# Low halves of expert weights: from GpSimd to VectorE

## The chip, the cores and the metric

The kernel runs on one core of a Trainium2 chip. The metric is the device time of one launch in microseconds (us); three runs were made, and their median counts. Times of single instructions come from one profiled execution and count from the start of its span. The engines are called by the profile's names: PE (TensorE, its matmuls), PEld (TensorE's weight loads), DVE (VectorE), ACT (ScalarE), POOL (GpSimd) and SP (SyncE, which here issues most transfers). A q behind a name is the engine's queue.

## The reference

Three stages follow one another; all of it is fp32.

```python
# 1. a linear attention over 768 steps, 4 batches x 8 heads, heads of 64
state = gamma * state + k[t] (outer) v[t];  y[t] = scale * q[t] @ state
x = y as 3072 rows of 512
# 2. a mixture of experts: one of 8 experts for each row
logits = x @ w_gate + modality_bias[modality_id];  e_idx = argmax(logits)
h = relu(x[mask] @ w1[e])            # 512 -> 1024
out[mask] = gate_w[mask] * (h @ w2[e])   # 1024 -> 512
# 3. a second layer of the same kind; its gate_w is multiplied by a sigmoid gate
```

The data decide which row goes to which expert, and so how many rows an expert gets.

## The kernel before, in words

**Three products for one.** An fp32 operand is split into a high half, which is the operand rounded to a shorter type, and a low half, the rest. A product is then made as high x high + high x low + low x high. For the weights, ACT writes the high half (`w1h`, `w2h`; lines 505 and 510), and another engine subtracts it from the raw weights (`w1l`, `w2l`; lines 506 and 511): `los[i].tensor_tensor(w1l[i][:, cols], raw1[i][:, cols], w1h[i][:, cols], op=ALU.subtract)`. Which engine this is comes from a list `los` with one engine for each of the four tiles of a matrix. x and the hidden values are split too: `xh` and `xl` (lines 545 and 547), `hh` and `hl` (882 and 883, or 903 and 904); their low halves are made on DVE.

**Slots.** After the routing the rows of one expert lie together in memory. A slot is a block of up to 256 rows of one expert; a layer has 12 to 19 slots, of which those that exist are run. A slot of 256 rows is run by `run` (full); one with at most 128 rows by `run_small` (small): the last block of an expert that doesn't fill a slot. PE's work in a full slot is `mm1` (line 891, eight steps f) and `mm2` (line 909, eight steps j); in a small slot `mm1s` (line 896, four steps), a transposition back (`htr`, line 902), and `mm2` in four steps.

**When weights change.** A register of the slot says whether its expert differs from the slot before (`chg`) and whether the next slot's will differ (`chgn`). If the next one differs, `split1(0)` and `split1(1)` make that expert's w1h and w1l during the second half of the current slot, by half rows: block 0 has the first 512 columns of each of four tiles, block 1 the rest. The w2 of a new expert is split in the slot that uses it: in a full slot all four tiles at its start (`split2`, all on DVE), in a small slot in pieces between the steps of mm1s. The raw weights of the expert after that are fetched by SP as soon as the raw tiles have been read. Each layer's first slot splits its w2 by a list of its own, written in `run`.

**Order.** Each engine works its instructions off in the order of the code. `at(j)` puts in the routing of the previous slot's results to layer 2, in steps: PE transposes `ob` (line 939) and makes the logits (945, 952), DVE copies them (947: `lT`; 954: `r_lg`) and finds each row's expert (lines 186 to 210: `r_oh`), PE counts (215), DVE places (221 to 260), and POOL scatters the rows (469). In layer 2, POOL scatters the results to the output (919). `xpose` (line 540, DVE) and `xsplit` (545 on ACT, 547 on DVE) prepare the next slot's x between split1(0) and split1(1). In a small slot the hl of the second half (line 904) stands between split1(0) and xpose on DVE.

The part of `run_small` around it reads:

```python
if j == 0:
    self.split1(0)
if j == 1:
    self.coming(nxt, Slot.xpose)
    self.coming(nxt, Slot.xsplit)
    self.split1(1)
```

Of the kernel before, what the change touches and what calls it, by code (L numbers as in the profile page):

```python
# [416 lines left out]
def retention_moe_moe_kernel(ctx: ExitStack, tc: tile.TileContext, q, k, v, mod, mb, wg, wg2, w1, w2, cst_d, out):  # L417
    nc = tc.nc
# [83 lines left out]
    def split1(los, ks=range(KD), half=None):  # L502
        cols = slice(0, F) if half is None else slice(half * F // 2, (half + 1) * F // 2)
        for i in ks:
            nc.scalar.activation(w1h[i][:, cols], raw1[i][:, cols], AF.Copy)  # L505
            los[i].tensor_tensor(w1l[i][:, cols], raw1[i][:, cols], w1h[i][:, cols], op=ALU.subtract)  # L506
# [96 lines left out]
    with ExitStack() as actx:  # L603
# [126 lines left out]
        for i in range(n):  # L730
# [17 lines left out]
            if n - 4 <= i < n - 1:  # L748
                split1([nc.gpsimd] * KD, [i - n + 4] if i < n - 2 else [2, 3])
# [39 lines left out]
    with ExitStack() as mctx:  # L789
# [28 lines left out]
        class Slot:  # L818
# [102 lines left out]

            def split1(self, half=None):
                with tc.If(self.chgn > 0):
                    split1([nc.vector, nc.gpsimd] * 2, half=half)

            def split2(self, ks=range(4), los=None):
                with tc.If(self.chg > 0):
# [109 lines left out]
            def run_small(self, steps=(), nxt=()):  # L1037

                at = self.steps(steps)
                self.ids(False)  # L1040
                los = [nc.vector] * (1 + (self.li == 2)) + [nc.gpsimd] * 3
                self.split2((0,) if self.li == 1 else (0, 1), los)
                for j in range(4):
                    if j == 3:
                        self.htr(0)
                    at(j)
                    if j:
                        self.split2((((1,), (2, 3), ()), ((), (2,), (3,)))[self.li - 1][j - 1], los)
                    self.mm1s(j // 2, (2 * (j % 2), 2 * (j % 2) + 1))
                    if j % 2:  # L1050
                        nc.scalar.activation(hs[:, (j // 2) * 512:(j // 2 + 1) * 512], hT[j // 2], AF.Relu)
                for j in range(4):
                    if j == 1:
                        self.htr(1)
                        self.prepare()
                    at(4 + j)
# [7 lines that stand above are left out]
                        nc.vector.memset(self.o[:, 0, W - 1:], 0.0)  # L1064
                        if self.li == 2:
                            nc.gpsimd.memset(self.o[:, 0, W - 1:], 0.0)
                    self.mm2(1, range(2 * j, 2 * j + 2), False)
                self.done(1)
                at(8)
# [137 lines left out]
```

## Time and profile before

| | us |
|---|---|
| median of three runs (lowest, highest) | 864.4 (864.32, 865.25) |
| the profiled execution's own time | 863.35 |
| its span, first to last instruction | 861.6 |
| PE busy with matmuls | 799.3 |
| DVE busy | 432.6 |
| POOL busy | 278.6 |
| ACT busy | 276.7 |

The span is from the first to the last instruction; 1.75 us of the execution's own time lie around it. The attention takes up the first part. From about 170 us on, the two layers run: 30 slots, 24 full and six small ones, by the counts of lines 891 and 896 (768 and 48 matmuls of each of their three kinds, 32 in a full slot and 8 in a small one). Matmuls overlap in the records, so that one begins before the one before it has ended; the step from row to row is what a matmul takes of PE's time.

### The profile page before, as it was taken

What the parts mean: (1) busy time and instruction counts of PE and PEld (TensorE: products, weight loads), DVE (VectorE), ACT (ScalarE), POOL (GpSimd) and SP (SyncE); (2) the same over time, 40 slices, a digit from 0 to 9 for tenths busy, and PEclk for the clock granted to TensorE, in tenths of its full rate; (3) what the DMA queues carried; (4) which work ended last, traced back from release to release, by engine and by line L of the source; (5) the groups of instructions that cost most, each with busy time, mean ns of one, the idle gap of its engine ahead of it and who ended that gap; (6) DMA issues with size and microseconds to landing.
All of it is one profiled execution on the core that took longest, in us unless ns stands there. A gap on an engine that the chain in (4) does not pass through costs nothing. (4 is left out here: it accounts for less than half of the span.)

```text
span 861.6 us, 18471 instructions
## 1 busy us (share of the span) xinstructions
PE 799.3 (93%) x5987; PEld 694.8 (81%) x5987; DVE 432.6 (50%) x1065; ACT 276.7 (32%) x476; POOL 278.6 (32%) x336
## 2 busy tenths in 40 slices
PE   8999998799999988999999599998999999999892
PEld 7788877788888967888888377797888888888671
DVE  4554456743444447333446675235454763635821
ACT  3444445311112224111114441115151651514610
POOL 3455456701122114122211752014231531323810
PEclk9999999999999999999999889999999999999997
DMA  9987899272111116211221714412635475343410
GB/s 171 232 219 183 181 230 311 89 246 71 52 39 39 39 28 202 74 52 52 74 66 27 225 37 138 137 59 70 213 98 179 129 249 164 120 155 113 149 40 16
DMA packets 149692, 107.02 MB, mean 124 GB/s; under 512 B 94845, under 2 KB 125693, under 8 KB 149504
## 3 DMA queue, kind: packets, MB, share of 16 engines
q1 hardware_dynamic: 141664, 85.37, 37.4%
q0 software_dynamic: 6400, 18.98, 6.0%
q8 instruction: 73, 1.20, 0.6%
q14 instruction: 115, 0.94, 0.4%
q10 hardware_dynamic: 1440, 0.53, 0.3%
HBM read 167.64 MB, written 25.83 MB: 225 GB/s over the span
## 5 line engine op out<-in xcount | busy, mean ns | idle before, releaser
L891 PE MATMUL hT<-xh,w1h 128*128 128x256 f32 x768 | 221.9, 289 | 2.0 <-ACT xh L545 1.6
L891 PE MATMUL hT<-xh,w1l 128*128 128x256 f32 x768 | 216.4, 282 | 3.9 <-POOL w1l L506 3.9
L891 PE MATMUL hT<-xl,w1h 128*128 128x256 f32 x768 | 216.4, 282 | 1.5 <-DVE xl L547 1.4
L909 PE MATMUL po<-w2l,hh 128*128 128x512 f32 x432 | 171.9, 398 | 2.1 <-POOL w2l L511 2.1
L909 PE MATMUL po<-w2h,hh 128*128 128x512 f32 x432 | 172.9, 400 | 0.3
L891 PEld LDWEIGHTS hT<-xh,w1h 128*128 128x128 f32 x768 | 145.9, 190 | 9.7 <-issue 5.6
L891 PEld LDWEIGHTS hT<-xh,w1l 128*128 128x128 f32 x768 | 145.7, 190 | 4.7 <-POOL w1l L506 4.7
L891 PEld LDWEIGHTS hT<-xl,w1h 128*128 128x128 f32 x768 | 146.0, 190 | 3.5 <-DVE xl L547 2.6
L909 PE MATMUL po<-w2h,hl 128*128 128x512 f32 x432 | 136.4, 397 | 1.4 <-DVE hl L904 1.4
L883 DVE SCALAR_TENSOR_TENSOR hl<-hT,hh 128x512 fp32r<-128x512 f32 x96 | 65.6, 690 | 133.3 <-ACT hh L882 106.4
L882 ACT ACTIVATE hh<-hT 128x512 fp32r<-128x512 f32 x96 | 57.2, 597 | 197.9 <-PE hT L891 177.9
L506 POOL TENSOR_TENSOR w1l<-raw,w1h 128x512 fp32r<-128x512 f32 (+1 forms) x44 | 70.9, 1630 | 114.4 <-ACT w1h L505 114.4
L909 PEld LDWEIGHTS po<-w2h,hl 128*128 128x128 f32 x432 | 81.4, 189 | 22.3 <-DVE hl L904 2.4
L909 PEld LDWEIGHTS po<-w2l,hh 128*128 128x128 f32 x432 | 81.7, 189 | 20.9 <-POOL w2l L511 2.9
L909 PEld LDWEIGHTS po<-w2h,hh 128*128 128x128 f32 x432 | 81.8, 189 | 19.7 <-ACT hh L903 1.6
L469 POOL DMA_INDIRECT x2d<-ob,r_idx x28 | 30.4, 1086 | 183.6 <-DVE ob L260 139.2
L919 POOL DMA_INDIRECT out_dram<-ob,to x28 | 30.9, 1102 | 148.2 <-DVE ob L917 93.1
L545 ACT ACTIVATE xh<-xTb 128x512 fp32r<-128x512 f32 x58 | 33.4, 624 | 97.6 <-DVE xTb L540 88.3
L547 DVE TENSOR_TENSOR xl<-xTb,xh 128x512 fp32r<-128x512 f32 x58 | 40.2, 734 | 22.0 <-ACT xh L545 22.0
L511 DVE TENSOR_TENSOR w2l<-raw,w2h 128x1024 fp32r<-128x1024 f32 x35 | 43.2, 1285 | 13.5 <-ACT hh L903 6.7
L540 DVE STREAM_TRANSPOSE xTb<-xqb 128x1024 f32<-128x1024 f32 x29 | 36.0, 1242 | 24.6 <-DMA xmb<-x2d 14.0
L505 ACT ACTIVATE w1h<-raw 128x512 fp32r<-128x512 f32 (+1 forms) x84 | 47.7, 640 | 0.0
(205 smaller groups left out, 1035.3 us busy)
## 6 DMA issues: line engine op xcount, KB each, us to landing
raw<-in_w_dram SPq DMA_DIRECT2D x248, 512.0 KB
xqb<-x2d SPq DMA_DIRECT2D x124, 64.0 KB
xqb<-x1d SPq DMA_DIRECT2D x108, 64.0 KB
nq<-in_q_dram SPq DMA_DIRECT2D x24, 256.0 KB
nk<-in_k_dram SPq DMA_DIRECT2D x24, 256.0 KB
nv<-in_v_dram SPq DMA_DIRECT2D x24, 256.0 KB
x1d<-zrow SPq DMA_DIRECT2D x4, 516.0 KB
x2d<-zrow SPq DMA_DIRECT2D x4, 516.0 KB
```

Source lines behind the costliest of these rows:

```text
L469: return nc.gpsimd.indirect_dma_start(out=dst, out_offset=bass.IndirectOffsetOnAxis(ap=rp.idx[:, t:t + 1], axis=0), in_=row, in_offset=Non ...
L505: nc.scalar.activation(w1h[i][:, cols], raw1[i][:, cols], AF.Copy)
L506: los[i].tensor_tensor(w1l[i][:, cols], raw1[i][:, cols], w1h[i][:, cols], op=ALU.subtract)
L511: los[i].tensor_tensor(w2l[i], raw2[i], w2h[i], op=ALU.subtract)
L540: nc.vector.transpose(xT.rearrange("p k (a i) -> p a k i", i=32), xq.rearrange("p a (k i) -> p a k i", k=KD))
L545: nc.scalar.activation(hi[:, k:k + 2, :], xT[:, k:k + 2, :], AF.Copy)
L547: nc.vector.tensor_tensor(lo[:, k:k + 2, :], xT[:, k:k + 2, :], hi[:, k:k + 2, :], op=ALU.subtract)
L882: nc.scalar.activation(hh[b], hT[b], AF.Relu)
L883: nc.vector.scalar_tensor_tensor(hl[b], in0=hT[b], scalar=0.0, in1=hh[b], op0=ALU.max, op1=ALU.subtract)
L891: nc.tensor.matmul(to, lhsT=a[k][:, fs], rhs=b[:, k, :], start=(k == 0 and m == 0), stop=(k == KD - 1 and m == 2))
L909: nc.tensor.matmul(po[h], lhsT=x[b][:, o:o + P], rhs=w[f // 2][:, f % 2, :], start=(f == 0 and i == 0), stop=(f == KF - 1 and x is hl))
L919: nc.gpsimd.indirect_dma_start(out=out, out_offset=bass.IndirectOffsetOnAxis(ap=to[:, t:t + 1], axis=0), in_=o[:, :DM], in_offset=None, bo ...
```

## The change

Two lists of engines are replaced. `split1` in a slot gave w1l of tiles 0 and 2 to DVE and of tiles 1 and 3 to POOL; now all four go to DVE. `run_small` gave w2l of tile 0 to DVE and of tiles 1 to 3 to POOL in layer 1, and of tiles 0 and 1 to DVE and 2 and 3 to POOL in layer 2; now all four go to DVE. What is subtracted from what, in which order on the code's page, and the w2 of each layer's first slot stay as they are; so does the split of the first expert's w1 during the attention, which POOL makes.

```diff
             def split1(self, half=None):
                 with tc.If(self.chgn > 0):
-                    split1([nc.vector, nc.gpsimd] * 2, half=half)
+                    split1([nc.vector] * 4, half=half)
...
                 self.ids(False)
-                los = [nc.vector] * (1 + (self.li == 2)) + [nc.gpsimd] * 3
+                los = [nc.vector] * 4
                 self.split2((0,) if self.li == 1 else (0, 1), los)
```

DVE's queue in a small slot of layer 1, from the first split of w2 to the first hl. In the names, w2l_104 to w2l_107 are the low halves of w2's four tiles, w2h_100 to w2h_103 the high ones, raw_88 to raw_91 the raw weights.

```order
 L927 COMPARE_AND_BRANCH
+L511 TENSOR_TENSOR w2l_105<-raw_89,w2h_101 128x1024
 L927 UNCONDITIONAL_BRANCH x2
 L947 COPY lT_2161<-misc 128x256
 L927 COMPARE_AND_BRANCH
+L511 TENSOR_TENSOR w2l_106<-raw_90,w2h_102 128x1024
+L511 TENSOR_TENSOR w2l_107<-raw_91,w2h_103 128x1024
 L927 UNCONDITIONAL_BRANCH x2
 L904 TENSOR_TENSOR hl_2147<-hT_118,hh_2143 128x512
```

One subtraction stands ahead of lT now, and two more ahead of the first hl and of the routing behind it. They stood on POOL's queue.

DVE's queue in the same slot, block 0 of w1 (w1l_96 to w1l_99 are the low halves of its four tiles, w1h_92 to w1h_95 the high ones):

```order
 L923 COMPARE_AND_BRANCH
 L506 TENSOR_TENSOR w1l_96<-raw_84,w1h_92 128x512
-L506 TENSOR_TENSOR w1l_98<-raw_86,w1h_94 128x512
+L506 TENSOR_TENSOR w1l_97<-raw_85,w1h_93 128x512
+L506 TENSOR_TENSOR w1l_98<-raw_86,w1h_94 128x512
+L506 TENSOR_TENSOR w1l_99<-raw_87,w1h_95 128x512
 L923 UNCONDITIONAL_BRANCH x2
 L904 TENSOR_TENSOR hl_2148<-hT_119,hh_2144 128x512
```

Four half rows instead of two stand ahead of the second hl.

DVE's queue in a small slot of layer 2, from the third tile of w2 to the second hl, with the same names:

```order
+L511 TENSOR_TENSOR w2l_106<-raw_90,w2h_102 128x1024
 L927 UNCONDITIONAL_BRANCH x2
 L904 TENSOR_TENSOR hl_2147<-hT_118,hh_2143 128x512
 L927 COMPARE_AND_BRANCH
-L927 UNCONDITIONAL_BRANCH x2
-L923 COMPARE_AND_BRANCH
-L506 TENSOR_TENSOR w1l_96<-raw_84,w1h_92 128x512
-L506 TENSOR_TENSOR w1l_98<-raw_86,w1h_94 128x512
+L511 TENSOR_TENSOR w2l_107<-raw_91,w2h_103 128x1024
+L927 UNCONDITIONAL_BRANCH x2
+L923 COMPARE_AND_BRANCH
+L506 TENSOR_TENSOR w1l_96<-raw_84,w1h_92 128x512
```

Here one w2l stands ahead of the first hl, and one more ahead of block 0 of w1.

## Rows read from the trace of the kernel before

**Rows 1.** Page, part 1: busy us, share of the span, instructions.
```profile
PE 799.3 (93%) x5987; PEld 694.8 (81%) x5987; DVE 432.6 (50%) x1065; ACT 276.7 (32%) x476; POOL 278.6 (32%) x336
```

**Rows 2.** Waits of PE: line, waited for, us in total, times, longest.
```profile
PE misc L215 <- DVE r_oh L210: 11.0, 3, 7.3
...
PE hT L891 <- POOL w1l L506: 3.9, 4, 1.4
...
PE po L909 <- POOL w2l L511: 2.1, 2, 1.4
```

**Rows 3.** Groups by form on POOL: count, busy us, mean ns, idle before.
```profile
L506 POOL TENSOR_TENSOR w1l<-raw,w1h 128x512 fp32r<-128x512 f32 x40 | 61.5, 1557 | 110.1 <-ACT w1h L505 110.1
...
L511 POOL TENSOR_TENSOR w2l<-raw,w2h 128x1024 fp32r<-128x1024 f32 x9 | 22.4, 2506 | 0.3 <-ACT w1h L505 0.3
```

**Rows 4.** Timeline of DVE and POOL, layer 1's last slot: start, us, engine, line.
```profile
484.37 1.23 DVE L511 TENSOR_TENSOR w2l<-raw,w2h 128x1024 fp32r<-128x1024 f32 x1 [6.71 <-ACT hh L903]
485.51 0.42 DVE L947 COPY lT<-misc 128x256 f32<-128x256 f32 x1
...
488.12 2.21 DVE L193 TENSOR_SCALAR rdz<-r_lg 128x16 f32<-128x16 f32 x1
490.24 2.38 DVE L277 SCALAR_TENSOR_TENSOR sct<-sct,smx,cst 128x8 f32<-128x8 f32 x1
...
485.61 6.99 POOL L511 TENSOR_TENSOR w2l<-raw,w2h 128x1024 fp32r<-128x1024 f32 x3
```

**Rows 5.** Timeline of PE, rows with a wait (in brackets), and one before.
```profile
322.83 0.73 PE L909 MATMUL po<-w2h,hl 128*128 128x512 f32 x2 [1.43 <-DVE hl L904]
...
485.99 0.62 PE L952 MATMUL misc<-cst,lT 128*128 128x16 f32 x4 [2.71 <-DVE lT L947]
...
495.48 0.17 PE L215 MATMUL misc<-r_oh,cb 128*128 128x16 bf16 x1 [7.28 <-DVE r_oh L210]
...
598.04 0.28 PE L891 MATMUL hT<-xl,w1h 128*128 128x256 f32 x1
599.22 0.38 PE L891 MATMUL hT<-xh,w1l 128*128 128x256 f32 x1 [0.90 <-POOL w1l L506]
...
802.98 0.50 PE L909 MATMUL po<-w2l,hh 128*128 128x512 f32 x1 [1.44 <-POOL w2l L511]
```

**Rows 6.** Timeline of DVE, the routing's chain in a full slot, first and last.
```profile
460.74 0.18 DVE L954 COPY r_lg<-misc 128x32 f32<-128x32 f32 x1
...
462.46 0.17 DVE L210 TENSOR_TENSOR r_oh<-r_oh,valid 128x16 bf16<-128x16 bf16 x1
```

**Rows 7.** Timeline of DVE, the first small slot with a change.
```profile
318.07 1.29 DVE L236 CAST r_idx<-rrk 128x2 uint32<-128x2 f32 x1
...
319.39 1.22 DVE L239 TENSOR_SCALAR rrm<-r_idx 128x2 uint32<-128x2 uint32 x1
...
320.89 1.29 DVE L506 TENSOR_TENSOR w1l<-raw,w1h 128x512 fp32r<-128x512 f32 x2
322.10 0.68 DVE L904 TENSOR_TENSOR hl<-hT,hh 128x512 fp32r<-128x512 f32 x1
```

**Rows 8.** Timeline of ACT and DVE, block 0 in a small slot of layer 2.
```profile
590.55 2.18 ACT L505 ACTIVATE w1h<-raw 128x512 fp32r<-128x512 f32 x4
591.20 0.69 DVE L506 TENSOR_TENSOR w1l<-raw,w1h 128x512 fp32r<-128x512 f32 x1 [1.24 <-ACT w1h L505]
...
593.55 0.68 DVE L904 TENSOR_TENSOR hl<-hT,hh 128x512 fp32r<-128x512 f32 x1
```

**Rows 9.** Timeline of DVE, block 0 and hl of the one-slot expert.
```profile
798.98 0.69 DVE L506 TENSOR_TENSOR w1l<-raw,w1h 128x512 fp32r<-128x512 f32 x1 [1.26 <-ACT w1h L505]
...
801.02 0.69 DVE L904 TENSOR_TENSOR hl<-hT,hh 128x512 fp32r<-128x512 f32 x1 [0.32 <-ACT hh L903]
```

**Rows 10.** Stretch by engine: us, busy (instructions), granted clock, DMA share, GB/s.
```profile
495.40:500.00 4.60, 4.52 (x16) 3.64 (x16) 3.44 (x23) 0.58 (x1) 0.00 (x0) 0.50 0.13 49
```

**Rows 11.** Timeline of DVE, the end of a full slot without a change.
```profile
378.03 0.75 DVE L915 TENSOR_SCALAR ob<-po,xmb 128x512 f32<-128x512 f32 x1 [4.84 <-PE po L909]
```

## The prediction

> **What bounds the kernel now.** I read the page first: TensorE (PE) is busy for 93% of the span, VectorE (DVE) for 50%, GpSimd (POOL) for 32% [rows 1]. Of so busy an engine the question is only what its idle time waits for, so the list of waits came next. The reader is to see there that PE waits for POOL's own results six times, 6.0 us in all (3.9 for w1l, 2.1 for w2l), and that the longest entry, 11.0 us in three waits, is for r_oh, which DVE makes [rows 2]. The groups by form then give POOL's price: 1557 ns for a half row of w1l, 2506 ns for a w2l [rows 3]. Last came the timelines of the stretches around the waits. There the reader is to see that DVE's small operations beside a POOL subtraction grow from below 0.2 us to 1 to 2.4 us (the subtraction at 488.12 takes 2.21 us and the next 2.38, while POOL makes three w2l from 485.61 to 492.60) [rows 4], where the same chain in a quiet slot has rows of 0.17 us [rows 6]. So POOL costs PE time twice: where PE waits for POOL, and where DVE stands behind POOL and PE behind DVE.
>
> **What moves.** 40 half rows of w1l (20 blocks of two, so ten changes of expert) and five of the nine w2l in rows 3: three in layer 1's last slot (rows 4), two in the one-slot expert at 798 us; the other four belong to the layers' first slots and stay. A DVE half row alone takes 0.69 us and the next begins 0.605 later (two in 1.21 us, 320.89 to 322.10) [rows 7]; a DVE w2l gives way to its successor after 1.14 us (484.37 to 485.51) [rows 4]. So DVE takes on 40 x 0.605 + 5 x 1.14 = 29.9 us, and POOL loses 40 x 1.56 + 5 x 2.5 = 75 us. DVE works in order: what stands behind each block is hl (for the next matmuls), the transposition of the next slot's x, and the next block.
>
> The profile shows no quiet half row in blocks of four, so pace has two ends: ScalarE makes four w1h in 2.18 us, one each 0.545 [rows 8], and DVE needs 0.605. With the later of them a block of four lasts 4 x 0.605 = 2.42 us. Before, from the first half row to the hl behind the second, delayed one, it lasted 593.55 - 591.20 = 2.35 us [rows 8]. A block of four on DVE alone therefore ends 0.07 us later than two beside POOL.
>
> **Full slots, five changes.** PE waits for nothing there. The 0.1 us per block lies under the second half of the slot: DVE then stands idle for 4.84 us until the slot's last bank is ready [rows 11]. Should the jump over a longer block cost more than it does now, that same idle time covers it up to 4.84 us. Cost 0.
>
> **First small slot with a change (318 us).** The casts at 318.07 and 319.39 take 1.29 and 1.22 us beside POOL; at 0.17 us each they give back 2.17, so the block starts at 318.72, lasts 2.42 and hl starts at 321.14 instead of 322.10 [rows 7]. PE waits for that hl until 322.83, idle for 1.43 us [rows 5]: 0.96 is gone. The block behind it is paced by ScalarE as above, 0.07 later. Gain 0.9; bounds 0 (hl late for another reason) and 1.4 (the whole wait).
>
> **Layer 1's last slot (484 us).** Now w2l[0] at 484.37, then w2l[1], which is new, to 486.65; lT at 486.65, so PE's first wait, to 485.99 [rows 5], grows by 1.14. Then w2l[2] and w2l[3] from about 487.0 to 489.3, hl to 489.9, and the routing chain, which from the logits' copy to the end of r_oh takes 462.63 - 460.74 = 1.89 us where POOL is quiet [rows 6]: 491.8. PE resumed at 495.48 [rows 5]. That is 3.6 earlier; 0.3 off for the branches of two blocks that now hold work: gain 3.3. Bounds: 0 if the three w2l in the queue eat the gain; 7.3, the whole wait.
>
> The clock adds a little: PE's granted clock is 0.50 from 495.4 to 500 [rows 10], the 1.2 GHz level, after PE had stood still twice. Half of these 4.6 us, 2.3, is the most that a shorter wait can return; 0 is the least. PE still waits twice for over 2 us, so I take 0.3.
>
> The long operation at 490.24 ends at 492.62, and POOL's third w2l at 492.60 [rows 4]: it stood until POOL let go. In the Trainium skill, "SBUF — State Buffer", section "Who interferes with whom", says that a DVE operation with two SBUF inputs, or in a two-port mode, and a GpSimd operation that reads SBUF exclude each other for a whole instruction; the later one waits. By that rule the excess goes entirely with POOL's w2l and the sum below stands; if the length were DVE's own, the rival "Slower" below would hold, at 867.6. The two ends, 0.02 us apart, speak for the rule.
>
> **Two small slots of layer 2 (597 and 679 us).** PE waits 0.90 us for POOL's w1l; from row to row it is 599.22 - 598.04 = 1.18 us [rows 5], of which the matmul before has some part, so I take 1.0 as lost. On DVE these half rows stand ahead of xl, for which PE waits anyway, so the wait goes. The hl before is 0.07 later. Gain 2 x (1.0 - 0.07) = 1.9 for both; bounds 1.6 (the idle time less 0.1) and 2.1.
>
> **The one-slot expert (798 to 811 us).** Four waits on POOL: all of w2l's 2.1 us, and of w1l's 3.9 what the two slots above leave, 2.1 [rows 2]; the first is in rows 5 (802.98). With some 0.2 each until matmuls follow closely again (1.18 - 0.90 = 0.28 at most), 5.0 us. Against it DVE takes two w2l (2.28) and two half rows (1.21) ahead of the hl at 801.02, where it now idles 1.26 ahead of the block and 0.32 before hl [rows 9], and about as long in between; hl comes some 0.6 later, at 801.6, and with it the transposition and xl. PE then waits about 0.2 for hl and 0.5 for xl. Gain 4.3; bounds 5.0, with no new wait, and 3.0, with two of 1.0 us each.
>
> **Sum.** 0.9 + 3.3 + 0.3 + 1.9 + 4.3 = 10.7 us off the profiled execution: 863.35 - 10.7 = 852.65. That execution lies 1.05 us below the median 864.4 of the runs, so 853.7 is predicted. Elsewhere DVE was behind nothing of POOL's that PE waited for. Raw loads that waited for POOL's reads are released earlier, never later. What becomes late next is r_oh again (its own chain), then xl behind its transposition.
>
> **The rivals.**
> - *The wait only changes hands.* At each place DVE's queue is about as late as POOL was: the gain at 484 us is 0.5 and that of the one-slot expert its lower bound less refills, 2.2; with 0.9 and 1.6 that makes 5.2, so 859.2. For it: three w2l in front of the routing. Against: POOL's three take 6.99 us, DVE's 3 x 1.14 = 3.4.
> - *Slower.* DVE's long small operations are not POOL's doing, so nothing is given back and the work comes on top. 318 us: 1.21 ahead of hl, and again ahead of the routing's input, +2.4; 484 us: 3 x 1.14, +3.4; layer 2's two slots: 1.21 - 1.0 each, +0.4; one-slot expert -3.0. Together +3.2: 867.6. It decides if the 2.21 and 2.38 us operations keep over 1 us. Against it: the whole chain, these operations in it, takes 1.89 us in the quiet slot [rows 6].
> - *The clock stays up.* With the wait at 484 us short enough that the 1.2 GHz level isn't granted, 2.0 more is gained: 851.7. Against: two waits remain.
> - *Nothing.* ScalarE's w1h pace and DVE's late arrival at 484.37, after 6.71 us without work [rows 4], set the same ends whoever subtracts: 864.4 within 0.2%. Against: PE's six waits end on POOL itself.
>
> **How the numbers follow.** Forecast 0.70; wait changes hands 0.12; clock 0.10; nothing 0.04; slower 0.04. Two runs of this kernel differ by up to 0.1%, so 0.2% (1.7 us) is what can be told from no change. Faster by more: 0.70 + 0.12 + 0.10 = 0.92; same 0.04; slower 0.04. The range from the bounds: least gain 0 + 0.5 + 0 + 1.6 + 3.0 = 5.1, which is 859.3; greatest, with most of the long wait (5.5) and half the clock's return (1.2), 1.4 + 5.5 + 1.2 + 2.1 + 5.0 = 15.2, cut to 14.4 since not all fall together: 850.0. I leave the two tails of slower and nothing, and a little of each end, outside: 850.0 to 859.3.
>
> **What would show it.** In the profile after: POOL busy about 75 us less, with no w1l of 128x512 left; no PE wait on POOL's w1l or w2l; in layer 1's last slot r_oh ready 3 to 4 us earlier, its chain's rows at 0.17 us, w2l four times on DVE; PE's wait for lT there longer by about 1.1; DVE's half rows at 0.69 us throughout. I am wrong if the chain's rows stay above 1 us, if PE takes up new waits for hl or xl of over 1 us in small slots, or if full slots begin to wait.

## The result and the profile after

The changed kernel takes 853.8 us (median of 853.39, 853.74, 853.79 and 856.8), the kernel before 864.8 beside it (864.32 to 868.85): a ratio of 0.987, 95% interval 0.983 to 0.991. Predicted were 853.7 us and 850.0 to 859.3. The profiled execution took 853.39 us (span 851.5); that of before, 863.35 (861.6).

Part 1 of the page stands against [rows 1]:

```profile
PE 799.0 (94%) x5987; PEld 696.2 (82%) x5987; DVE 430.3 (51%) x1110; ACT 276.2 (32%) x476; POOL 202.1 (24%) x291
```

POOL lost 76.5 us of work (75 predicted). DVE took on 45 instructions and is busy 2.3 us *less*. The groups by form say why. The first row below is the kernel before's, the others are the changed kernel's; the POOL row answers to the second of [rows 3], and there is no POOL w1l of 128x512 left:

```profile
L506 DVE TENSOR_TENSOR w1l<-raw,w1h 128x512 fp32r<-128x512 f32 x40 | 41.9, 1054 | 7.8 <-ACT w1h L505 7.8
```

```profile
L506 DVE TENSOR_TENSOR w1l<-raw,w1h 128x512 fp32r<-128x512 f32 x80 | 49.8, 683 | 2.5 <-ACT w1h L505 2.5
L511 DVE TENSOR_TENSOR w2l<-raw,w2h 128x1024 fp32r<-128x1024 f32 x40 | 47.3, 1234 | 13.7 <-DMA xqb<-x1d 6.2 <-ACT w2h L510 4.8 <-issue 2.6
...
L511 POOL TENSOR_TENSOR w2l<-raw,w2h 128x1024 fp32r<-128x1024 f32 x4 | 10.5, 2633 | 9.1 <-ACT w2h L510 9.1
```

Before, DVE's own 40 half rows took 41.9 us, 1054 ns each; now 80 take 49.8, at 683. Twice the work costs 7.9 us more and five more w2l cost 4.1; DVE's other rows, no longer held up, give back some 14.

PE's waits stand against [rows 2]. Those on POOL's w1l and w2l are gone, r_oh (L210) has fallen from 11.0 to 6.3 us, and the second row and the last are new. The waits for r_oh behind L207, in the attention and in layer 1's first slot, rose from 4.7 to 6.0 us; the change leaves POOL's work there as it was:

```profile
PE misc L215 <- DVE r_oh L210: 6.3, 3, 2.6
...
PE hT L891 <- issue: 2.9, 1, 2.9
...
PE misc L952 <- DVE lT L947: 1.9, 1, 1.9
PE hT L891 <- ACT w1h L505: 1.7, 1, 1.7
```

The single waits on PE's timeline stand against [rows 5]; in brackets is the idle time before the row and what ended it:

```profile
322.23 0.74 PE L909 MATMUL po<-w2h,hl 128*128 128x512 f32 x2 [0.49 <-DVE hl L904]
...
481.48 0.64 PE L945 MATMUL misc<-oT,wgp 128*32 128x256 f32 x7 [1.21 <-issue]
486.03 0.62 PE L952 MATMUL misc<-cst,lT 128*128 128x16 f32 x4 [1.88 <-DVE lT L947]
490.70 0.17 PE L215 MATMUL misc<-r_oh,cb 128*128 128x16 bf16 x1 [2.58 <-DVE r_oh L210]
500.38 0.36 PE L891 MATMUL hT<-xh,w1h 128*128 128x256 f32 x1 [1.75 <-ACT w1h L505]
532.61 0.57 PE L891 MATMUL hT<-xh,w1h 128*128 128x256 f32 x1 [2.92 <-issue]
593.46 0.38 PE L891 MATMUL hT<-xl,w1h 128*128 128x256 f32 x1 [0.34 <-DVE xl L547]
799.29 0.38 PE L891 MATMUL hT<-xl,w1h 128*128 128x256 f32 x1 [0.34 <-DVE xl L547]
```

The wait at L945, which nothing in the profile releases, is new too.

Where the time came from is read by matching PE's instructions between the two traces and noting by how much each starts earlier or later; the growth of that shift over a stretch is the stretch's gain.

| stretch (times of before) | predicted | measured |
|---|---|---|
| first small slot, 318 us | -0.9 | -0.9 |
| layer 1's last slot to its end, 480 to 507 | -3.6 (with the clock) | -4.1 |
| layer 2's first slot, 507 to 523 | 0 | -0.4 |
| layer 2's second slot, 523 to 575 | 0 | **+1.5** |
| two small slots, 597 and 679 | -1.9 | -2.0 |
| one-slot expert, 798 | -4.3 | -4.4 |
| start and tail | 0 | -0.1 |
| sum | -10.7 | -10.4 |

DVE's timeline of layer 1's last slot stands against [rows 4]:

```profile
483.28 2.36 DVE L511 TENSOR_TENSOR w2l<-raw,w2h 128x1024 fp32r<-128x1024 f32 x2 [6.22 <-DMA xqb<-x1d]
485.55 0.42 DVE L947 COPY lT<-misc 128x256 f32<-128x256 f32 x1
485.89 2.35 DVE L511 TENSOR_TENSOR w2l<-raw,w2h 128x1024 fp32r<-128x1024 f32 x2
...
489.34 0.16 DVE L193 TENSOR_SCALAR rdz<-r_lg 128x16 f32<-128x16 f32 x1
489.45 0.23 DVE L277 SCALAR_TENSOR_TENSOR sct<-sct,smx,cst 128x8 f32<-128x8 f32 x1
490.48 0.17 DVE L210 TENSOR_TENSOR r_oh<-r_oh,valid 128x16 bf16<-128x16 bf16 x1
492.86 2.50 DVE L506 TENSOR_TENSOR w1l<-raw,w1h 128x512 fp32r<-128x512 f32 x4
...
499.08 2.49 DVE L506 TENSOR_TENSOR w1l<-raw,w1h 128x512 fp32r<-128x512 f32 x4
```

Four w2l stand in DVE's queue where one stood, and PE still has r_oh 4.8 us earlier: L193 and L277 take 0.16 and 0.23 us where they took 2.21 and 2.38. The blocks of four w1l last 2.50 us: three pitches of 0.605 and a last row of 0.68.

### The profile page after: what moved, and what is told of

It is laid out like the page before. It is cut to its first block, busy times and chain, and to the rows that moved or that the text cites. A ratio compares the mean times of both kernels' runs of the same rounds, so it can differ in the third digit from the quotient of the medians.

```text
span 851.5 us, 18413 instructions
## 1 busy us (share of the span) xinstructions
PE 799.0 (94%) x5987; PEld 696.2 (82%) x5987; DVE 430.3 (51%) x1110; ACT 276.2 (32%) x476; POOL 202.1 (24%) x291
## 5 line engine op out<-in xcount | busy, mean ns | idle before, releaser
L891 PE MATMUL hT<-xh,w1h 128*128 128x256 f32 x768 | 222.4, 290 | 4.7 <-issue 2.9
L891 PE MATMUL hT<-xl,w1h 128*128 128x256 f32 x768 | 216.7, 282 | 1.4 <-DVE xl L547 1.4
L891 PE MATMUL hT<-xh,w1l 128*128 128x256 f32 x768 | 216.5, 282 | 0.0
L891 PEld LDWEIGHTS hT<-xh,w1h 128*128 128x128 f32 x768 | 146.4, 191 | 12.4 <-issue 11.0
L891 PEld LDWEIGHTS hT<-xl,w1h 128*128 128x128 f32 x768 | 146.6, 191 | 2.9 <-DVE xl L547 2.2
L891 PEld LDWEIGHTS hT<-xh,w1l 128*128 128x128 f32 x768 | 146.4, 191 | 0.0
L511 DVE TENSOR_TENSOR w2l<-raw,w2h 128x1024 fp32r<-128x1024 f32 x40 | 47.3, 1234 | 13.7 <-DMA xqb<-x1d 6.2
L506 DVE TENSOR_TENSOR w1l<-raw,w1h 128x512 fp32r<-128x512 f32 x80 | 49.8, 683 | 2.5 <-ACT w1h L505 2.5
L547 DVE TENSOR_TENSOR xl<-xTb,xh 128x512 fp32r<-128x512 f32 x58 | 37.6, 690 | 22.3 <-ACT xh L545 22.3
L915 DVE TENSOR_SCALAR ob<-po,xmb 128x512 f32<-128x512 f32 x24 | 18.0, 750 | 54.5 <-PE po L909 54.5
```

Source lines behind the costliest of these rows:

```text
L511: los[i].tensor_tensor(w2l[i], raw2[i], w2h[i], op=ALU.subtract)
L547: nc.vector.tensor_tensor(lo[:, k:k + 2, :], xT[:, k:k + 2, :], hi[:, k:k + 2, :], op=ALU.subtract)
L891: nc.tensor.matmul(to, lhsT=a[k][:, fs], rhs=b[:, k, :], start=(k == 0 and m == 0), stop=(k == KD - 1 and m == 2))
L915: nc.vector.tensor_scalar(perm(o[:, :DM]), plain(po[h]), gate, None, op0=ALU.mult)
```

## The experiments

Each ratio is to runs of the kernel before on the same chip (there 865.4 to 867.5 us in the median, so absolute times lie some 1 to 3 us higher than the expectations reckoned). In the single profiles PE's first matmuls after the attention come 0.7 us earlier to 3.8 later than before, whatever the kernel, so stretches behind that point are compared.

**The exclusion, by shadow work.** Theory: a POOL subtraction and a DVE instruction keep each other out, and that, not only PE's waits on POOL's results, cost the time. Rival: DVE's long rows were its own, or came of waiting for results. The first kernel leaves all that the program uses on DVE and lets POOL repeat its former work for nobody (here and in the next two kernels the calls of small helpers are written out):

```diff
 split1([nc.vector] * 4, half=half)
+for i in (1, 3):
+    nc.gpsimd.tensor_tensor(junk[:, half, :], raw1[i][:, cols], w1h[i][:, cols], op=ALU.subtract)
...
 split2(los or [nc.vector] * 4, ks)
+if los:    # small slots only
+    for i in [k for k in ks if k > (self.li == 2)]:
+        nc.gpsimd.tensor_tensor(junk, raw2[i], w2h[i], op=ALU.subtract)
```

> The changed kernel, and GpSimd makes its former subtractions as well, from the same inputs into a scratch tile (bf16, for its size) that nothing reads; VectorE makes all that the program uses. Theory (exclusion): VectorE's blocks of four take about 4 us again in place of 2.50 and the r_oh wait at 490 comes back to 5 us or more; no PE wait on GpSimd's w1l or w2l, yet the time is as before or longer, since VectorE has more to do than before and is held up as much: 862 to 872, best guess 866. Rival (VectorE was late only because it waited for GpSimd's results or queue): 853 to 855.

Measured: 881.95 us, ratio 1.015 (1.012 to 1.019): slower than before, and by 10 us more than my range allowed. The first row below is the group by form of DVE's half rows, the others are the timeline of layer 1's last slot:

```profile
L506 DVE TENSOR_TENSOR w1l<-raw,w1h 128x512 fp32r<-128x512 f32 x80 | 90.2, 1187 | 2.5 <-ACT w1h L505 2.5
```

```profile
498.51 4.75 POOL L522 TENSOR_TENSOR junk<-raw,w2h 128x1024 bf16<-128x1024 f32 x2
498.57 2.31 DVE L201 SCALAR_TENSOR_TENSOR rq<-rdz,cst 128x16 f32<-128x16 f32 x1
...
501.00 2.28 DVE L284 TENSOR_TENSOR sto<-sto,r_first 128x1 f32<-128x1 f32 x1
...
504.76 0.17 PE L215 MATMUL misc<-r_oh,cb 128*128 128x16 bf16 x1 [9.52 <-DVE r_oh L210]
```

Two POOL operations run back to back, and DVE's chain lets through one long row beside each, though nothing waits for a result of POOL. L284 works on one element per partition and takes 2.28 us, where it takes 0.16 in the changed kernel. The rival is out. That the size was off because 80 half rows, not 40, are now held up, by 0.5 us each, and the small slots' hl and xl with them, fits the profile (PE waits 7.5 us for hl and 4.1 for xl in all), but no run tests it.

The next two put other POOL work in the same places: copies that read one tensor, and memsets that read none (shown for w1; for w2 there are five of each in place of three).

```diff
-    nc.gpsimd.tensor_tensor(junk[:, half, :], raw1[i][:, cols], w1h[i][:, cols], op=ALU.subtract)
+    for _ in range(3):
+        nc.gpsimd.tensor_copy(junk, w1h[i][:, cols])    # the copies
...
+    nc.gpsimd.tensor_copy(junk[:, :1], w1h[i][:, cols][:, :1])
+    for _ in range(3):
+        nc.gpsimd.memset(junk, 0.0)                     # the memsets
```

> The changed kernel with other shadow work: in place of each subtraction that GpSimd repeated, it copies w1h (three times 128x512) or w2h (five times) into a scratch tile that nothing reads: one input from SBUF instead of two. If any GpSimd read of SBUF keeps a two-input VectorE operation out, VectorE's half rows of w1l, 0.68 us each in the changed kernel and 1.19 with the subtractions, stay near 1 us or more, and the time is 865 to 885. If only GpSimd operations with two inputs do, they are at 0.7 and the time is 853 to 858.

> The same, but GpSimd only writes: a copy of one column (so that it starts at the same moment) and three or five memsets of 128x512, 0.52 us each in the changed kernel's profile, so about as much GpSimd time as the subtractions took. If the exclusion is over reads of SBUF, VectorE's half rows stay at 0.68 to 0.75 us and the time is 853 to 859; if over GpSimd's access to SBUF of any kind, they are at 0.9 or more and the time is 862 to 880.

Measured: copies 867.1 us, ratio 1.0005 (0.998 to 1.003); memsets 856.25, ratio 0.988 (0.984 to 0.992), which is the changed kernel's own. The groups by form, DVE and POOL, of the copies and then of the memsets:

```profile
L506 DVE TENSOR_TENSOR w1l<-raw,w1h 128x512 fp32r<-128x512 f32 x80 | 74.0, 984 | 2.5 <-ACT w1h L505 2.5
...
L519 POOL COPY junk<-w1h 128x512 f32<-128x512 f32 x120 | 99.4, 829 | 97.1 <-ACT w1h L505 90.8
```

```profile
L506 DVE TENSOR_TENSOR w1l<-raw,w1h 128x512 fp32r<-128x512 f32 x80 | 49.8, 684 | 2.5 <-ACT w1h L505 2.5
...
L520 POOL MEMSET junk<- 128x512 f32 x120 | 63.2, 527 | 7.0
```

63 us of POOL writes leave DVE's half rows at 684 ns; reads of one tensor put them at 984 and eat the whole gain (the copies keep POOL busy longer than the subtractions of the first shadow kernel did, yet cost less). So it is POOL's reads of SBUF that cost the half rows their time. The Trainium skill, "SBUF — State Buffer", section "Who interferes with whom", says just this of a DVE instruction with two SBUF inputs: it contends with a GpSimd instruction that reads SBUF, not with one that only writes. These two runs agree.

Beside memsets some small rows of the routing grew all the same, the one below from 0.17 us to 0.55. From the start of L210 to the next w1l DVE takes 3.06 us there, where it takes 2.38 in the changed kernel; why these rows and not the half rows, no run shows.

```profile
493.97 0.55 DVE L239 TENSOR_SCALAR rrm<-r_idx 128x2 uint32<-128x2 uint32 x1
...
493.39 2.86 POOL L526 MEMSET junk<- 128x512 f32 x5
```

**Each edit alone.**

```diff
 # w1l alone: the first edit as it is, the second undone
-los = [nc.vector] * 4
+los = [nc.vector] * (1 + (self.li == 2)) + [nc.gpsimd] * 3
 # w2l alone: the second edit as it is, the first undone
-split1([nc.vector] * 4, half=half)
+split1([nc.vector, nc.gpsimd] * 2, half=half)
```

> Only the first of the two edits is made: w1l is all VectorE's, the small slots' w2l stay mostly GpSimd's. Theory (a GpSimd subtraction and a VectorE instruction keep each other out for whole instructions, so GpSimd's work costs the PE twice: through its own late results and through VectorE's held-up chains): layer 1's small slot at 318 us gains its 0.9, layer 2's small slots their 2.0, and of layer 1's last slot (484) and the one-slot expert (798) only about half, 2 and 2.4 us, since w2l still runs on GpSimd there: about 857, range 855.5 to 858.5. Rival (only waits of the PE on GpSimd's own results count): 0.9 + 0.9 + 1.35 + the hl wait 0.9 = 4: about 860.5.

> Only the second edit is made: the small slots' w2l are all VectorE's, half of w1l stays GpSimd's in every slot. Theory: layer 1's last slot gains 2.5 of its 3.5 (the r_oh wait of 7.28 falls to about 3.5), the one-slot expert about 3 (the w2l wait of 1.44 and VectorE's hold-ups before it), the small slots at 318, 597 and 679 nothing, so those POOL w1l waits of 0.9 stay: about 858.8, range 857 to 860.5. Rival (direct waits only): 1.44 alone: about 863.

Measured: w1l alone 856.74 us, ratio 0.987 (0.984 to 0.991); w2l alone 856.26, 0.986 (0.983 to 0.990). The ratios don't tell the three kernels apart; their intervals are some 6 us wide. From 172 us on the single profiles give 8.9 us for w1l, 7.5 for w2l and 10.8 for both. PE's waits, w1l alone and then w2l alone:

```profile
493.52 0.17 PE L215 MATMUL misc<-r_oh,cb 128*128 128x16 bf16 x1 [1.25 <-DVE r_oh L210]
503.00 0.36 PE L891 MATMUL hT<-xh,w1h 128*128 128x256 f32 x1 [2.05 <-ACT w1h L505]
...
799.72 0.79 PE L909 MATMUL po<-w2l,hh 128*128 128x512 f32 x1 [2.95 <-POOL w2l L511]
```

```profile
491.20 0.17 PE L215 MATMUL misc<-r_oh,cb 128*128 128x16 bf16 x1 [1.45 <-DVE r_oh L210]
...
500.92 0.36 PE L891 MATMUL hT<-xh,w1h 128*128 128x256 f32 x1 [1.60 <-ACT w1h L505]
596.56 0.39 PE L891 MATMUL hT<-xh,w1l 128*128 128x256 f32 x1 [0.90 <-POOL w1l L506]
```

I had shared each place out between the edits, and that was wrong. At layer 1's last slot either edit takes the r_oh wait from 7.28 to about 1.3, and then the next slot waits 1.6 to 2.1 us for w1h: a floor that both edits together meet too (1.75). At the one-slot expert it is the other way round: w1l alone loses 0.8 there (POOL's w2l comes later still), w2l alone gains 1.2, both gain 4.4. Part of what both runs gain at 484 us (4.9 for w1l alone and 7.5 for w2l alone, against 4.1 for both) is no gain: PE came 3 to 4 us late to that slot, and its wait for lT, 2.71 before, is 1.15 in the one and gone in the other, since what lT waits for did not come as late.

**The rest of POOL's w2l**, two in each layer's first slot, which the change left:

```diff
-split2([nc.gpsimd] * 2 + [nc.vector] * 2, ({0: (2, 0, 1), 1: (3,)}, {1: (2, 0), 2: (1, 3)})[self.li - 1].get(f, ()))
+split2([nc.vector] * 4, ({0: (2, 0, 1), 1: (3,)}, {1: (2, 0), 2: (1, 3)})[self.li - 1].get(f, ()))
```

> The changed kernel, and the two w2l that GpSimd still makes in each layer's first slot go to VectorE too, at the same places in the program. Theory: the VectorE rows of the routing beside them (4.57 us at 161.6, 1.74 and 1.32 at 509 to 511.6) fall to their undisturbed 0.2 to 1.3, but two subtractions of about 1.2 us each now stand ahead of them in VectorE's queue, so the r_oh waits of 3.98 and 2.63 fall by 1 to 2 and by 0 to 1: about 851.8, range 850.5 to 853.5. Rival (the queue costs as much as the exclusion did): 853.8, up to 855.

Measured: 847.45 us, ratio 0.976 (0.972 to 0.980). This beats both kernels, by more than I expected. DVE and POOL in layer 1's first slot, in the changed kernel and then here:

```profile
161.50 4.67 POOL L511 TENSOR_TENSOR w2l<-raw,w2h 128x1024 fp32r<-128x1024 f32 x2
161.63 4.57 DVE L190 TENSOR_TENSOR rdz<-r_lg,rmx 128x16 f32<-128x16 f32 x1
```

```profile
158.35 3.50 DVE L511 TENSOR_TENSOR w2l<-raw,w2h 128x1024 fp32r<-128x1024 f32 x3 [0.96 <-ACT w2h L510]
...
166.06 0.17 DVE L190 TENSOR_TENSOR rdz<-r_lg,rmx 128x16 f32<-128x16 f32 x1
```

PE's wait of 3.98 us behind L190 is gone entirely, and with it a stretch at a lower clock, as the windows of the two show:

```profile
168.00:172.00 4.00, 4.00 (x27) 4.00 (x26) 3.35 (x29) 0.60 (x1) 2.06 (x2) 0.68 0.17 66
```

```profile
168.00:172.00 4.00, 4.00 (x33) 3.87 (x32) 3.83 (x34) 1.09 (x2) 1.78 (x2) 1.00 0.12 46
```

From the first matmul of L891 at 153 to 172 us this kernel gains 4.4 where the changed one loses 0.3; layer 2's first slot gives 2.3 against 0.4.

**What bounds layer 1's last slot now?** Two kernels on top of the last one. One moves two w2l behind the routing, the other makes the second half of w1h before xh on ScalarE:

```diff
-self.split2((((1,), (2, 3), ()), ((), (2,), (3,)))[self.li - 1][j - 1], los)
+self.split2((((1,), (), (2, 3)), ((), (2,), (3,)))[self.li - 1][j - 1], los)
```

```diff
+self.split1(1, "h")     # ScalarE's w1h alone
 self.coming(nxt, Slot.xpose)
 self.coming(nxt, Slot.xsplit)
-self.split1(1)
+self.split1(1, "l")     # VectorE's w1l alone
```

> On the kernel with first slots on VectorE: in layer 1's small slots two of the four w2l subtractions move behind the routing's short instructions in VectorE's queue. Both theories expect the r_oh wait of 2.58 at layer 1's last slot to fall to about 0.3. If that wait sets the slot's end, 2 us are gained. If VectorE's queue as a whole sets it (it works from 483 to 502 without a gap over 0.8, and the next slot's first matmul waits 1.75 to 2.5 us for w1h), the wait at about 500 grows by as much and nothing is gained, within 0.5 us. I expect the second.

> On the kernel with first slots on VectorE: in the small slots ScalarE makes the second half of the next expert's w1h ahead of the next slot's xh, not behind it; VectorE's order stays. If the wait for w1h at about 500 us (2.53) is ScalarE's own order, it falls to about 1 and 1 to 1.5 us are gained there; what is left is the wait for w1l, VectorE's next in turn. If VectorE's queue sets it (xTf, then xl, then w1l), the first w1l is at 499.1 as before and at most 1 us is gained. The extra branch per slot may cost some tenths of a us in every slot.

Measured: 847.53 us, ratio 0.978 (0.975 to 0.981), and 844.81, ratio 0.976 (0.973 to 0.978); neither can be told from the 0.976 they started from. PE in the slot, w2l behind the routing and then w1h ahead:

```profile
486.95 0.17 PE L215 MATMUL misc<-r_oh,cb 128*128 128x16 bf16 x1 [0.50 <-DVE r_oh L210]
...
494.59 1.22 PE L909 MATMUL po<-w2h,hl 128*128 128x512 f32 x2 [2.36 <-DVE hl L904]
499.20 0.55 PE L891 MATMUL hT<-xh,w1h 128*128 128x256 f32 x1 [0.83 <-ACT w1h L505]
```

```profile
495.72 0.36 PE L893 MATMUL hT<-xh,w1h 128*128 128x256 f32 x1 [1.90 <-issue]
```

In the first, r_oh's wait falls as both theories said, but hl, behind the moved w2l in DVE's queue, is late by as much, PE's granted clock is 0.50 from 496 to 500, and the stretch 480 to 507 gains only 1.3 where it gained 4.3. Here DVE's queue sets the slot's end: what was moved in it came back as another wait. In the second the w1h wait goes, and in its place is one of 1.90 that nothing in the profile releases; what bounds the slot's end then is open.

**The attention's w1l**, on the same base:

```diff
-split1([nc.gpsimd] * KD, [i - n + 4] if i < n - 2 else [2, 3])
+split1([nc.vector] * KD, [i - n + 4] if i < n - 2 else [2, 3])
```

> On the kernel with first slots on VectorE: the first expert's four w1l (1024 columns each), made on GpSimd in the last three steps of the attention, go to VectorE. Theory (exclusion): the VectorE row that lasts 2.07 us beside GpSimd's 4.68 at 147 to 152 falls to 0.2, the r_oh wait of 2.06 behind it goes, and 1 to 2.5 us are gained. Rival (an in-order queue): VectorE now stands still until ScalarE has made each w1h, which GpSimd did for it, and the attention's own VectorE work behind it is late: 1 to 3 us slower.

Measured: 848.67 us, ratio 0.980 (0.977 to 0.983): no gain. L190 falls from 2.07 to 0.17, yet PE's r_oh wait only from 2.06 to 1.69: the two w1l now stand ahead of it on DVE (2.36 us from 147.41). Here queue and exclusion cost about the same.

**The wait that I had not foreseen** (2.92 at 532.61) is no POOL matter. First the changed kernel again, word for word:

> The changed kernel once more, word for word the same, to see what of its profile recurs. If the PE's wait of 2.92 us that nothing in the profile releases (532.6, start of layer 2's second slot) belongs to how this program's code lies, it is there again; if it belongs to one execution, it is gone or elsewhere, and the program is then up to 2 us shorter at 575 us. The ratio to the kernel before should be 0.987 again, within 0.985 to 0.990, though its absolute time may lie 2 to 3 us higher, as all four kernels of the last set showed their first matmuls after the attention 3 to 4 us later than before and after did.

Measured: 855.09 us, ratio 0.986 (0.984 to 0.989), and the wait is there again:

```profile
535.37 0.57 PE L891 MATMUL hT<-xh,w1h 128*128 128x256 f32 x1 [2.88 <-issue]
```

Of the twelve profiles up to here (the expectation below says ten kernels; before, after and ten runs are meant) five have such a wait: those in which SyncE's weight loads began 4.7 to 6.0 us before PE's last row (of two matmuls) of the slot before; in the other seven it is 3.4 at most. So the loads were held back in the changed kernel:

```diff
 if first and j == 5:
     self.regs()
+    if self.li == 2:
+        nc.sync.dma_start(junk[:, 0:1], self.o[:, 0, 0:1])
+        nc.sync.dma_start(junk[:, 1:2], junk[:, 0:1])
     self.load(raw1, w1)
```

> The changed kernel, and in layer 2's first slot SyncE's weight loads wait for two small transfers in a chain, the first of which needs VectorE's result of 524.9 us, so that they start about 3 us later than at 524.4; all else is the same. In ten kernels so far PE entered layer 2's second slot with a wait of 2.8 to 3.5 us that nothing in the profile releases whenever those loads had begun 4.7 to 6.0 us before its last matmul of the slot before (five kernels), and without it when they began at most 3.4 us before (seven). If the loads in flight make that wait (PE's next code comes by DMA too), it falls below 1 us and the kernel is 1.5 to 2.5 us shorter than the changed one at 575 us. If it is only a matter of how the program lies, the wait stays at 2.8 to 3. Should the delayed weights be late for their own use, a new wait of ScalarE's w1h or w2h shows within the next 25 us.

Measured: 856.58 us, ratio 0.989 (0.986 to 0.992). The timeline's row of those weight loads in the changed kernel; then here, with PE's waits:

```profile
524.36 19.14 SPq L500 DMA_DIRECT2D raw<-in_w_dram  x12
```

```profile
529.65 0.38 PE L893 MATMUL hT<-xh,w1h 128*128 128x256 f32 x1 [0.47 <-ACTq L925]
530.11 17.78 SPq L500 DMA_DIRECT2D raw<-in_w_dram  x12
...
559.05 0.58 PE L893 MATMUL hT<-xh,w1h 128*128 128x256 f32 x1 [6.74 <-ACT xh L547]
```

The loads begin 5.8 us later, and the wait is gone: at this slot, loads in flight make it. They don't everywhere. In the changed kernel layer 1's second slot begins at 184.01 without a wait, though twelve weight loads began at 177.78, 5.8 us before the last row ahead of it. That it is PE's code which comes late is an inference, and the traces fit it. In each of the thirteen profiles a transfer of 16 KB on DMA queue 8, of the kind "instruction", starts shortly ahead of the slot: in the five with the wait 0.3 to 0.5 us before PE's last matmul ends, in the other seven 2.6 to 3.2 us, with the loads held back 3.1. Whose code the queue carries, no run shows. And there was nothing to win: a new wait of 6.74 for the next slot's xh ends 28.9 us after the loads began. In the kernel before that distance is 29.0 (530.49 to 559.48), in six of the other kernels 28.6 to 30.1: the third slot's x comes behind these loads on SyncE's queue. Loads that start early stall PE ahead of this slot; late ones delay x.

## Why the prediction was right

- *Reading POOL twice*, through PE's waits on it and through DVE's held-up chains, was the step that carried the number, and the shadow kernels show it. Of the measured 10.4 us, 5.0 lie at layer 1's two places, where PE waited only for DVE.
- *Durations.* Half rows of 0.605 us pitch, w2l of 1.14 and casts of 0.17 all came out; first small slot, two small slots and the one-slot expert are within 0.1 us of their terms. "Two of 1.0 us each", the lower bound there, did not come: xl waits 0.34.
- *Layer 1's last slot*: 3.6 forecast, 4.1 measured, but not from my terms alone. DVE's chain came out: from the start of w2l[0] to the end of r_oh it took 7.37 us (483.28 to 490.65) where I had worked out 7.43 (484.37 to 491.8). It began 1.1 us earlier; PE was 0.6 us ahead by then, and where the rest comes from no run shows. PE's wait for lT was to grow by 1.14 and shrank, 2.71 to 1.88, for a reason that I had not seen: lT was ready as before (at 485.97, before at 485.93), but PE came to it 0.9 us later, after the new wait of 1.21 at L945. PE resumed behind r_oh 4.8 us earlier. Then the next slot waited 1.75 for w1h, which I had not on my list of what is late next.
- *The clock term* (0.3) was too small: the half-level stretch ends near 494.6, against [rows 10], and from r_oh to 501.6 us (times of before), where PE waits in neither kernel, its lead grows by 1.15. The wait of 1.75 for w1h behind it, which I had missed, took more than that away again.

```profile
492.00:494.60 2.60, 2.60 (x9) 2.10 (x9) 2.60 (x12) 0.81 (x2) 0.95 (x1) 0.50 0.21 79
494.60:500.00 5.40, 4.04 (x17) 2.87 (x15) 4.64 (x8) 2.93 (x7) 2.43 (x6) 0.98 0.27 94
```

- *"Full slots, cost 0"* failed in one place: layer 2's second slot lost 1.5. I looked at DVE's idle time there, not at when the loads begin: 6.1 us earlier than before (530.49 to 524.36), where PE's last matmul ahead of the slot came 4.7 earlier. I had written of loads that they come "earlier, never later", as if early were free. By my own list of signs ("if full slots begin to wait") I was wrong here.
- *"Elsewhere DVE was behind nothing of POOL's that PE waited for"* was wrong. In layer 1's first slot of the kernel before, DVE's L183 takes 4.79 us (from 162.09) beside two w2l of POOL (162.15 to 166.84), and PE waits 2.60 us for r_oh behind it. The sum didn't suffer, since the change leaves these w2l; but the kernel that moves them too has the ratio 0.976 against 0.987.
- The rivals "slower" and "nothing" are out, and "the clock stays up" too: the clock was 0.50 from 492.0 to 494.6. "The wait changes hands" was true in part: 1.75 of what r_oh gave up went to w1h, and each edit alone already met that wait.
- *That the median fell within 0.1 us of 853.7* is luck. The places were off by 0.5 and 0.4 one way and by 1.5 the other, and the changed kernel's own runs spread over 3.4 us. The 0.1% that I took for noise, from three runs, was too little: runs of the kernel before, here and beside the experiments, lie between 861.96 and 873.17.

## What to carry to other kernels

Before GpSimd is given a subtraction as help, look for VectorE rows that are long beside it: its price is VectorE's chain as well as its own 1.5 to 2.5 us. Work that only writes cost little beside it here. When a wait goes, ask what starts earlier with it, the loads above all, and try each edit alone, since two edits can pay for the same wait.

## What the runs showed of the hardware

- A VectorE instruction of one element per partition (L284) took 2.28 us beside one GpSimd subtraction (GpSimd's shadow work), 0.16 without.
- In these kernels GpSimd's copies, which read one tensor, cost VectorE's half rows of w1l 0.30 us each on average (684 to 984 ns), its subtractions, which read two, 0.50 (1187), and its memsets nothing (684), though a TENSOR_SCALAR and a CAST of two elements per partition took 0.55 us beside a memset, 0.17 without.
- At layer 2's second slot, weight loads begun at least 4.7 us before PE's last row of the slot before went with a wait of 2.8 to 3.5 us ahead of PE's next matmul (five profiles), begun at most 3.4 us before they did not (seven); holding them back took the wait away. At layer 1's second slot loads begun 5.8 us before it made none.
